# First products copied into the bank of the second product, gate rows on another engine, and loads and forms at other steps

## The chip, the cores and the metric

The kernel runs on one core of a Trainium2 chip. The core has a matrix engine (TensorE, PE in the profile; its weight loads are listed apart as PEld), a vector engine (VectorE, DVE), a scalar engine (ScalarE, ACT), GpSimd (POOL, used here to issue stores) and SyncE (SP, used here to issue loads). Each engine works through its own instruction queue; they wait for each other by semaphores. The metric is the time of one execution on the device in microseconds (us), the median of several runs.

## The reference, cut to what matters

```python
g = sigmoid((x * gate_w).sum(-1, keepdims=True))          # x: 2048 x 512
a = x @ hid_re.T ; b = x @ hid_im.T                       # hid: 512 x 512
fourier = seq_re @ a - seq_im @ b                         # seq: 2048 x 2048
swiglu = (silu(x @ w1) * (x @ w3)) @ w2                   # w1, w3: 512 x 1376
return g * fourier + (1 - g) * swiglu
```

All of it is float32.

## The kernel before, in words

**Products.** Each large product is taken as a 2 x 2 block product by seven block multiplications with sums of blocks in front and behind (a Strassen-Winograd scheme). Each float32 operand is split into a high part (rounded to fp32r, `high`, a ScalarE copy) and a low part (`low`, a VectorE subtraction: source minus high). One block product is then three matmuls: high x high, high x low, low x high (`mm3`, line 122). The first matmul of a product needs the high part of the moving operand, the second its low part.

**Stage one** (lines 345 to 405, to about 208 us) computes silu(x w1) and x w3 for 22 items n, an item being 128 of the hidden columns and one half of the rows of x. An item has seven products of six matmuls. X is the bank of the first product (weights `wa`, x form B11). The first and second products of item n + 3 are taken during item n (LOOK = 3): `first1` makes X, and ScalarE copies X into the SBUF tile s1 (`copy_x`, line 291). Two products later `first2` makes the second product in its own bank Y (one of two), VectorE adds Y to s1 (`sum_g`, line 305), and ScalarE applies Silu to s1 (`gate1`, line 309). The X bank keeps the first product and gets others added to it. The weights of the back half of the items are loaded a second time, `load_w` for `wa` and `load_wb` for `wb`; ScalarE makes the high part of `wa`, VectorE the low. Items 0 to 3 have a start written out by hand (lines 409 to 515).

The order of all instructions is the order in which the Python code is written; nothing reorders it. Functions are put into lists (`early`, `ahead`, `second`, `mid`, `at_end`) that `gate_up` runs at fixed points of an item.

**Stage two** (from line 627) has eight blocks: four of the Fourier product (kind F, 28 steps each), two of kind H (the product with w2, 21 steps) and two of kind Y (the hidden Fourier matrices, 14 steps). A step is a quarter, a third or a half of one of the seven products P1, P5, P6, P3, P7, P2, P4 and has twelve matmuls (six where half a form is empty). Its moving operand is the tile zo of that step (high and low). While TensorE works on step m, `advance(m)` issues the load for step m + 8, the sum (line 682 or 685) for step m + 4 and the split into zo for step m + 3. There are four zo tiles, so VectorE and ScalarE can be three steps ahead.

The stationary operands of the F blocks are forms of x: A1 (made in stage one) and A2, eight tiles a2_0 to a2_7, made from eight reloaded x tiles xs during block 0. For each p of them there is one subtraction of 128 x 256 (`sum2`, line 174), and a split of two parts: "first" forms (512 wide) and a "third" form (256 wide, from the result of that subtraction). P7 (steps 16 to 19) reads the third forms, P2 and P4 (steps 20 to 27) the first ones. In the kernel before, the subtraction for p stands at step 7 + p and the split of both parts at step 8 + p.

When a product ends its banks are read: P1 into s1, P5 into p5, P6 into u2, P7 into u3 by ScalarE; results of P3, P2, P4 and P7 are summed, multiplied with the gate by VectorE and stored (`spill`, from line 811). The P3 result of block 0 is worked off at step 18. The gate rows themselves (`gates`) are made from the scores at step 4 of block 0 and step 3 of block 1. Six matrices (two of w2, four of the hidden Fourier matrix) are turned into forms "late", two in each of blocks 1, 2 and 3 (`late_load`, `late_sums`, `late_split1`, `late_split2`), and stored to memory for blocks 4 to 7.

Of the kernel before, what the change touches and what calls it, by code (L numbers as in the profile page):

```python
# [7 lines left out]
F32 = mybir.dt.float32  # L8
# [20 lines left out]
A1_AT = (12, 14, 16, 17, 18, 19, 20)  # L29


@with_exitstack
def fnet_swiglu_gate_kernel(
# [142 lines left out]
    def forms2(r, t2):  # L176

        r = r.rearrange("p (a n) -> p a n", a=4)
        split(flat(t2[:, 0, 0:2]), flat(t2[:, 1, 0:2]), flat(r[:, 2:4]))
        split(t2[:, 0, 2], t2[:, 1, 2], r[:, 0])  # L180

# [99 lines left out]
    def first1(n):  # L281
        copy_x(n, prod1(n))
# [6 lines left out]
    def copy_x(n, x):  # L289
        s1 = s1p.tile([P, 512], F32, tag="s1", name=f"s1_{n}")  # L290
        nc.scalar.activation(s1, x, AF.Copy)
        G[n] = (x, s1)

    def first2(n):

        sum_g(n, prod2(n))

    def prod2(n):
        y = bank(4 + n % 2, f"Y{n}")
        prod(y, n, 1, 1, True)  # L300
        return y

    def sum_g(n, y):
        s1 = G[n][1]
        nc.vector.tensor_add(s1, s1, y)
        put_score(n, 0, s1)

    def gate1(n):
        nc.scalar.activation(G[n][1], G[n][1], AF.Silu)
# [35 lines left out]
    def gate_up(n):  # L345
# [17 lines left out]
        if wa in WA or wa == 0:  # L363
            wa = None
        else:
            load_w(wa, 0, 3 if back(wa) else 4)

# [44 lines left out]
    wps = bank(7, "wps")  # L412
# [82 lines left out]
    y1 = prod2(1)  # L495
    copy_x(1, x1)
    nc.vector.tensor_mul(h0[:, 512:], g1, C[1, 1])
    store_h(0, 1, h0[:, 512:])
    x2 = prod1(2)
    high_wb(1)  # L500
    sum_g(1, y1)
    y2 = prod2(2)
    low(*wa_parts(3, 0, 3))
    copy_x(2, x2)
    sum_xo(0, "T3", ST[0, "B12"])
    gate1(1)
    x3 = prod1(3)
    low_wb(1)
    high(*xo_parts(0, "T3")[::2])
    y3 = prod2(3)  # L510
    copy_x(3, x3)
# [12 lines left out]
    do(second, 1, sum_g, 2, y2)  # L524
    do(mid, 1, gate1, 2)
    do(early, 2, sum_g, 3, y3)
    do(mid, 2, gate1, 3)
# [200 lines left out]
    def load_a2(p):  # L728
# [5 lines left out]
        elif p < NG - 2:  # L734
            XR[p] = flat(ut.tile([P, 2, 512], F32, tag=("u3", "c21")[p % 2], name=f"xs{p}"))
# [13 lines left out]
    def load_score(g):  # L749
        t, ng = GATES[g] = [flat(ut.tile([P, 2, 512], F32, tag=k, name=f"{k}g{g}"))  # L750
                            for k in ("p5", "u2")]
# [8 lines left out]
    def gates(g):  # L760

        t, ng = GATES.pop(g)
        nc.scalar.activation(t, t, AF.Sigmoid)
        for j, (v, w) in enumerate(((-1.0, 1.0), (1.0, -1.0))):
            b = slice(j * 512, (j + 1) * 512)
            nc.vector.tensor_scalar(ng[:, b].rearrange("p (n a) -> p a n", a=2),
                                    t[:, b].rearrange("p (a n) -> p a n", a=2),
                                    v, w, op0=ALU.mult, op1=ALU.add)
        nc.scalar.activation(t[:, 512:], t[:, 512:], AF.Copy, scale=-1.0)
        nc.gpsimd.dma_start(gsp[g], t)  # L770
        nc.gpsimd.dma_start(ngsp[g], ng)
# [100 lines left out]

    def step(m):
# [4 lines left out]
        if q == 0 and k in ("P1", "P5", "P2"):  # L878
            banks = {"P1": XB[blk % 2], "P5": ZB, "P2": YB}[k]
            U[k] = [bank(b, f"{k}_{blk}_{r}") for r, b in enumerate(banks)]  # L880
# [3 lines left out]
        own = k in ("P1", "P5", "P2")  # L884
# [46 lines left out]
        if k == "P1":  # L931
# [5 lines left out]
        elif k == "P3":  # L937
# [4 lines left out]
            result() if blk else todo.setdefault(m + 3, []).append((result, ()))  # L942
        elif k == "P7":
# [6 lines left out]
            spill(blk, 3, U["p5"])  # L950
        elif k == "P2":
# [114 lines left out]
```

## Time and profile before

| | |
|---|---|
| median of the runs | 679.93 us (679.02, 679.96, 679.93) |
| span of the profiled execution, first to last instruction | 678.0 us |
| outside the span, median less span | 1.93 us |
| mean granted TensorE clock | 1.000 |
| PE / PEld / DVE / ACT / POOL busy | 671.4 / 583.1 / 601.9 / 367.1 / 64.0 us |
| memory traffic | 172.5 MB, mean 254 GB/s |

The profiled execution's own time is not listed apart from its span; the 1.93 us are taken as what lies around it. In the profile a line L122 is line 122 of the kernel; helpers give all their instructions one line (L108 all high parts, L111 all low parts, L122 all matmuls but the warm-up). A row of a timeline has start and duration in us, engine, line, operation, output<-input, size, count, and in square brackets the idle time before it and what ended it. A row of waits has the sum in us, how often, and the longest. A row of windows has, for PE, PEld, DVE, ACT and POOL, the busy time in us, then the granted clock, the share of the memory engines that was busy, and GB/s.

### The profile page before, as it was taken

The numbers are of one execution on the slowest core, as the hardware profiler recorded it, in microseconds if no ns is written. First come the engines' busy times: TensorE is split into PE (matmuls) and PEld (weight loads), VectorE is DVE, ScalarE is ACT, GpSimd is POOL, SyncE is SP. The second block draws the span as 40 slices with busy tenths as digits, with TensorE's granted clock in tenths as the row PEclk, the third lists the DMA queues.
The fourth block names the chain that finished last, engine by engine and source line by source line (L and its number), as shares of the span: only waits on it lengthen the run. The fifth ranks groups of instructions, "written<-read, shape, count | busy, mean of one in ns | idle before, by whom it ended". The sixth has DMA issues, their size and how long they took to land.

```text
span 678.0 us, 8653 instructions
## 1 busy us (share of the span) xinstructions
PE 671.4 (99%) x3101; PEld 583.1 (86%) x3101; DVE 601.9 (89%) x738; ACT 367.1 (54%) x480; POOL 64.0 (9%) x118
## 2 busy tenths in 40 slices
PE   9999999999999999999999999999999999999997
PEld 6888888888888888888888888888888888888886
DVE  6999988787679999987999799979998897898995
ACT  6665566654546754454554554555546455455452
POOL 0021112221010000000110001100110000000000
PEclk9999999999999999999999999999999999999999
DMA  7675557599998656912497238915999972874932
GB/s 294 218 294 219 219 203 267 198 325 380 415 418 295 242 189 232 339 64 93 165 380 278 94 105 332 376 58 199 373 418 417 414 272 90 310 284 153 336 127 93
DMA packets 45547, 172.54 MB, mean 254 GB/s; under 512 B 5312, under 2 KB 5696, under 8 KB 41664
## 3 DMA queue, kind: packets, MB, share of 16 engines
q1 hardware_dynamic: 32608, 118.63, 48.0%
q0 software_dynamic: 12608, 52.97, 19.6%
q8 instruction: 24, 0.39, 0.2%
q10 hardware_dynamic: 288, 0.39, 0.2%
q14 instruction: 19, 0.16, 0.1%
HBM read 114.82 MB, written 57.16 MB: 254 GB/s over the span
## 4 chain that ended last, share of the span: by engine, by line
PE 51%; issue 37%; DMA 7%; POOL 3%; DVE 1%; ACT 0%; POOLq 0%; SPq 0%; ACTq 0%; DVEq 0%
PE P L122 24%; PE X L122 14%; PE Z L122 7%; PE Y L122 3%; DMA B<-hsp 2%; PE C L122 2%; DMA dsp<-late_0l 2%; DMA ws<-w 1%; DMA hsp<-h 1%; POOL zsp L821 1%; DMA p5g<-gs 1%; PE wps L414 1%; POOL dsp L803 1%; POOL w2sp L803 1%; DVE zo L111 0%
## 5 line engine op out<-in xcount | busy, mean ns | idle before, releaser
L122 PE MATMUL P<-zo,a 128*128 128x512 f32 x1344 | 290.8, 379 | 1.0 <-DVE zo L111 1.0
L122 PEld LDWEIGHTS P<-zo,a 128*128 128x128 f32 x1344 | 253.7, 189 | 38.0 <-DVE zo L111 2.0
L108 ACT ACTIVATE zo<-B 128x1024 fp32r<-128x1024 f32 (+1 forms) x182 | 188.4, 1041 | 180.5 <-DVE B L682 83.5
L111 DVE TENSOR_TENSOR zo<-B,zo 128x1024 fp32r<-128x1024 f32 (+1 forms) x182 | 217.2, 1200 | 30.9 <-ACT zo L108 30.2
L122 PE MATMUL P<-zo,H 128*128 128x512 f32 x468 | 101.4, 379 | 0.5 <-DVE zo L111 0.5
L122 PEld LDWEIGHTS P<-zo,H 128*128 128x128 f32 x468 | 88.4, 189 | 13.4 <-DVE zo L111 0.9
L682 DVE TENSOR_TENSOR B<-B,B 128x1024 f32<-128x1024 f32 (+1 forms) x78 | 92.7, 1189 | 1.5 <-DMA B<-hsp 1.4
L122 PE MATMUL X<-xo,wb 128*128 128x512 f32 x378 | 88.7, 379 | 0.0
L122 PEld LDWEIGHTS X<-xo,wb 128*128 128x128 f32 x378 | 71.2, 189 | 10.6 <-DVE u L382 0.3
L122 PE MATMUL P<-zo,Y 128*128 128x512 f32 (+1 forms) x336 | 71.6, 375 | 0.0
L122 PEld LDWEIGHTS P<-zo,Y 128*128 128x128 f32 x336 | 62.7, 189 | 8.7
L334 POOL DMA_DIRECT2D hsp<-h x42 | 23.0, 548 | 120.5 <-DVE h L388 66.3
L685 DVE TENSOR_TENSOR B<-B,B 128x1024 f32<-128x1024 f32 x26 | 31.6, 1216 | 0.0
L122 PE MATMUL X<-xo,wa 128*128 128x512 f32 x126 | 31.0, 381 | 0.3 <-ACT h L399 0.3
L122 PE MATMUL Y<-xo,wa 128*128 128x512 f32 x126 | 30.6, 379 | 0.0
L122 PE MATMUL Z<-xo,wb 128*128 128x512 f32 x126 | 30.6, 379 | 0.0
L122 PE MATMUL Z<-xo,wa 128*128 128x512 f32 x126 | 30.6, 379 | 0.0
L111 DVE TENSOR_TENSOR wa<-ws,wa 128x768 fp32r<-128x768 f32 (+1 forms) x22 | 19.3, 880 | 11.0 <-ACT wa L108 11.0
L925 ACT ACTIVATE zu<-P 128x512 f32<-128x512 f32 x32 | 19.0, 596 | 17.3 <-PE P L122 15.7
L122 PEld LDWEIGHTS X<-xo,wa 128*128 128x128 f32 x126 | 23.6, 189 | 4.5 <-ACT h L399 0.7
L122 PEld LDWEIGHTS Y<-xo,wa 128*128 128x128 f32 x126 | 23.8, 189 | 3.4
L122 PEld LDWEIGHTS Z<-xo,wb 128*128 128x128 f32 x126 | 23.8, 189 | 3.4
(140 smaller groups left out, 549.0 us busy)
## 6 DMA issues: line engine op xcount, KB each, us to landing
B<-cc SPq DMA_DIRECT2D x64, 512.0 KB, 6.4
hsp<-h POOLq DMA_DIRECT2D x42, 256.0 KB, 3.7
B<-hsp SPq DMA_DIRECT2D x20, 512.0 KB, 10.8
wbsp<-wb POOLq DMA_DIRECT2D x8, 1024.0 KB, 4.2
wb<-wbsp SPq DMA_DIRECT2D x8, 1024.0 KB, 8.1
B<-zsp SPq DMA_DIRECT2D x16, 512.0 KB, 8.3
H<-w2sp SPq DMA_DIRECT2D x6, 1024.0 KB, 9.3
ws<-w SPq DMA_DIRECT2D x11, 512.0 KB, 4.7
```

Source lines behind the costliest of these rows:

```text
L108: nc.scalar.activation(hi, src, AF.Copy)
L111: nc.vector.tensor_sub(lo, src, hi.bitcast(F32))
L122: nc.tensor.matmul(ps.rearrange("p (n a) -> p n a", a=2), u, turns(v)[:, some], **kw)
L334: nc.gpsimd.dma_start(hsp[g, b + k, j // 2, :, j % 2 * 512 : (j % 2 + 1) * 512], h)
L414: nc.tensor.matmul(wps, warm[:, :P], warm, start=True, stop=True)
L682: nc.vector.tensor_add(t, t, RAW[blk, b, q][:, :n])
L685: nc.vector.tensor_sub(t, RAW[blk, "B12", q], t)
L803: nc.gpsimd.dma_start(flat(dst[:, k]), v[:, : 1024 - 256 * j].bitcast(F32))
L821: return nc.gpsimd.dma_start(z_rows(blk, k), flat(t))
L925: nc.scalar.activation(U[name][:, r], ps[r], AF.Copy)
```

## The change

1. *Seeds.* ScalarE's copy of the first product goes into the bank Y of the second product (`seed`), and the second product is accumulated on it. `sum_g`'s addition goes; `gate1` reads Y. At the start, items 1 to 3 are ordered X1, X2, Y1, X3, Y2, Y3, and the warm-up matmuls use the bank 5. In stage two the P1 result of blocks 0 to 6 is copied into the two banks of P2 in the same way and `plus("s1")` goes; the multiplication with the gate (in block 6 the addition of nb) reads the banks.
2. *Gate rows.* The two rows of 1 - g and g - 1 are made by ScalarE, and the five instructions are spread over four steps (steps 2 to 5 of block 0, 3 to 6 of block 1).
3. *x forms.* A table gives, for each p, the step of its load, of its subtraction with the third form, and of its first form: subtraction and third form of p now stand together at steps 8 to 11 and 13 to 16, the first forms at 8 to 11, 17, 18, 18 and 19. P3's result of block 0 moves from step 18 to step 24.
4. *Late matrices and weights.* Blocks 1 and 2 take three late matrices each and block 3 none. The weights `wa` of the back half are loaded one item sooner.

```diff
+A2_AT = ((4, 8, 8), (5, 9, 9), (6, 10, 10), (7, 11, 11),
+         (8, 13, 17), (9, 14, 18), (10, 15, 18), (11, 16, 19))
...
-    def copy_x(n, x):
+    def seed(n, x):
+        y = bank(4 + n % 2, f"Y{n}")
+        nc.scalar.activation(y, x, AF.Copy)
+        G[n] = (x, y)
+
+    def first2(n):
+        prod(G[n][1], n, 1, 1, False, True)
+
+    def gate1(n):
+        x, y = G[n]
         s1 = s1p.tile([P, 512], F32, tag="s1", name=f"s1_{n}")
-        nc.scalar.activation(s1, x, AF.Copy)
+        nc.scalar.activation(s1, y, AF.Silu)
+        put_score(n, 0, y)
         G[n] = (x, s1)
-
-    def first2(n):
-        sum_g(n, prod2(n))
...
-    def sum_g(n, y):
-        s1 = G[n][1]
-        nc.vector.tensor_add(s1, s1, y)
-        put_score(n, 0, s1)
...
+        ask = WSET[n + LOOK + 2] if n + LOOK + 1 < last else 0
+        if back(ask) and ask not in WS:
+            load_w(ask, 0, 3)
...
-    def make_a2(p):
+    def third_a2(p):
         A2.append(a2.tile([P, 2, 3, 256], F32R, tag=f"a2_{p}", name=f"a2_{p}"))
-        r = XR.pop(p)
-        forms2(r, A2[p])
-        if p >= NG - 2:
+        r, t = XR[p], A2[p]
+        sum2(r)
+        split(t[:, 0, 2], t[:, 1, 2], r[:, :256])
+
+    def first_a2(p):
+        r, t = XR.pop(p), A2[p]
+        split(flat(t[:, 0, 0:2]), flat(t[:, 1, 0:2]), r[:, 512:])
+        if p >= NG - 1:
             free(r)
...
+        elif i < 3:
+            v = (1.0, -1.0)[i - 1]
+            b = slice((i - 1) * 512, i * 512)
+            nc.scalar.activation(ng[:, b].rearrange("p (n a) -> p a n", a=2),
+                                 t[:, b].rearrange("p (a n) -> p a n", a=2),
+                                 AF.Copy, bias=v, scale=-v)
...
-        if k == "P1":
+        if k == "P1" and seeded:
+            new_banks("P2", blk)
+            for r in range(2):
+                nc.scalar.activation(U["P2"][r], ps[r], AF.Copy)
+        elif k == "P1":
             read("s1")
...
-            result() if blk else todo.setdefault(m + 3, []).append((result, ()))
+            result() if blk else todo.setdefault(m + 9, []).append((result, ()))
...
+        elif k == "P2" and seeded:
+            spill(blk, 0, res("s1"), ps)
         elif k == "P2":
             plus("s1")
             spill(blk, 0, U["s1"])
...
-    for p in range(NG):
-        at(0, 4 + p, load_a2, p)
-
-        at(0, 7 + p, lambda p=p: sum2(XR[p]))
-    for p in range(NG):
-        at(0, 8 + p, make_a2, p)
+    for p, (load, third, rest) in enumerate(A2_AT):
+        at(0, load, load_a2, p)
+        at(0, third, third_a2, p)
+        at(0, rest, first_a2, p)
...
-        blk, b = 1 + i // 2, i % 2
-        n = (17, 24)[b]
-        at(blk, n - (5, 6)[b], late_load, i, src[p], ("u3", "u2")[b])
+        blk, b = 1 + i // 3, i % 3
+        n = (10, 17, 24)[b]
+        at(blk, n - (6, 5, 6)[b], late_load, i, src[p], ("u3", "s1", "u2")[b])
```

Where instructions move, three places. The first is VectorE in block 0, at the x forms that stand before the splits of steps 15 to 17 (xs is a reloaded x tile, a2 its form, B11 <- B12, B11 the sum of T3, zo the low part of a step). Before:

```order
L174 TENSOR_TENSOR xs5_2114<-xs5_2114 128x256
L111 TENSOR_TENSOR a2_4_2186<-xs4_2089,a2_4_2186 128x512
L111 TENSOR_TENSOR a2_4_2186<-xs4_2089,a2_4_2186 128x256
L685 TENSOR_TENSOR B11_0_0_1654<-B12_0_0_1886,B11_0_0_1654 128x1024
L111 TENSOR_TENSOR zo15_2206<-B22_0_3_1979,zo15_2206 128x1024
L174 TENSOR_TENSOR xs6_2137<-xs6_2137 128x256
L111 TENSOR_TENSOR a2_5_2210<-xs5_2114,a2_5_2210 128x512
L111 TENSOR_TENSOR a2_5_2210<-xs5_2114,a2_5_2210 128x256
L685 TENSOR_TENSOR B11_0_1_1726<-B12_0_1_1914,B11_0_1_1726 128x1024
L111 TENSOR_TENSOR zo16_2230<-B11_0_0_1654,zo16_2230 128x1024
```

And after:

```order
L113 TENSOR_TENSOR zo15_2179<-B22_0_3_1959,zo15_2179 128x1024
L176 TENSOR_TENSOR xs4_2073<-xs4_2073 128x256
L113 TENSOR_TENSOR a2_4_2182<-xs4_2073,a2_4_2182 128x256
L672 TENSOR_TENSOR B11_0_1_1705<-B12_0_1_1893,B11_0_1_1705 128x1024
L113 TENSOR_TENSOR zo16_2201<-B11_0_0_1634,zo16_2201 128x1024
L176 TENSOR_TENSOR xs5_2098<-xs5_2098 128x256
L113 TENSOR_TENSOR a2_5_2204<-xs5_2098,a2_5_2204 128x256
L672 TENSOR_TENSOR B11_0_2_1759<-B12_0_2_1895,B11_0_2_1759 128x1024
L113 TENSOR_TENSOR zo17_2223<-B11_0_1_1705,zo17_2223 128x1024
```

The subtraction xs of a p moved from the step ahead to the place right before the low part of its own third form, and the 512-wide low parts moved behind step 19.

The second is ScalarE in block 0 at steps 11 to 13, the high parts of the x forms and of zo. Before:

```order
L108 ACTIVATE a2_0_2091<-xs0_2004 128x512
L108 ACTIVATE a2_0_2091<-xs0_2004 128x256
L108 ACTIVATE zo11_2110<-B12_0_3_1918 128x1024
L108 ACTIVATE a2_1_2116<-xs1_2030 128x512
L108 ACTIVATE a2_1_2116<-xs1_2030 128x256
L108 ACTIVATE zo12_2133<-B22_0_0_1920 128x1024
```

And after:

```order
L110 ACTIVATE a2_0_2067<-xs0_1986 128x256
L110 ACTIVATE a2_0_2067<-xs0_1986 128x512
L110 ACTIVATE zo11_2089<-B12_0_3_1897 128x1024
L110 ACTIVATE a2_1_2092<-xs1_2007 128x256
L110 ACTIVATE a2_1_2092<-xs1_2007 128x512
L110 ACTIVATE zo12_2112<-B22_0_0_1899 128x1024
```

The copy of 256, which reads the result of the subtraction, moved ahead of the copy of 512.

The third is TensorE at the start of stage one. Before:

```order
L122 MATMUL X1_234<-xo0_109,wa1_219 128x512 x6
L122 MATMUL Y1_249<-xo0_109,wa1_219 128x512 x6
L122 MATMUL X2_260<-xo0_109,wa2_222 128x512 x6
L122 MATMUL Y2_270<-xo0_109,wa2_222 128x512 x6
L122 MATMUL X3_282<-xo0_109,wa3_247 128x512 x6
```

And after:

```order
L124 MATMUL X1_234<-xo0_109,wa1_219 128x512 x6
L124 MATMUL X2_249<-xo0_109,wa2_222 128x512 x6
L124 MATMUL Y1_256<-xo0_109,wa1_219 128x512 x6
L124 MATMUL X3_273<-xo0_109,wa3_247 128x512 x6
L124 MATMUL Y2_269<-xo0_109,wa2_222 128x512 x6
```

The second product of an item moved one product back.

More of the change, by code (lines that the diff above doesn't have):

```diff
@@ L281, in first1 @@
     def first1(n):
-        copy_x(n, prod1(n))
+        seed(n, prod1(n))
     def prod1(n):
@@ L758, in fnet_swiglu_gate_kernel, with gates @@
     load_score(0)
[L760 to L771, printed above, removed]
+    def gates(g, i):
+        t, ng = GATES[g]
+        if i == 0:
+            nc.scalar.activation(t, t, AF.Sigmoid)
+        elif i < 3:
[4 more added lines that the diff above has]
+                                 AF.Copy, bias=v, scale=-v)
+        else:
+            nc.scalar.activation(t[:, 512:], t[:, 512:], AF.Copy, scale=-1.0)
+            nc.gpsimd.dma_start(gsp[g], t)
+            nc.gpsimd.dma_start(ngsp[g], ng)
     LATE = {}
@@ L871, in load_forms, with new_banks @@
         nc.sync.dma_start(t.bitcast(F32), sp[j][p])
+    def new_banks(k, blk):
+        banks = {"P1": XB[blk % 2], "P5": ZB, "P2": YB}[k]
+        U[k] = [bank(b, f"{k}_{blk}_{r}") for r, b in enumerate(banks)]
     def step(m):
@@ L883, in step @@
         z = zt.rearrange("p h a n -> p h (a n)")
-        own = k in ("P1", "P5", "P2")
+        own = k in ("P1", "P5") or k == "P2" and not seeded
         first = k in ("P1", "P5", "P6", "P3")
```

61 lines of the change are left out of this document (25 added, 36 removed).

## The prediction

> **What bounds the kernel now.** I read the page's busy times first, then what the TensorE weight loads waited for, then those waits in order of time, then VectorE and ScalarE around them. The head of the page:
>
> ```profile
> span 678.0 us, 8653 instructions
> PE 671.4 (99%) x3101; PEld 583.1 (86%) x3101; DVE 601.9 (89%) x738; ACT 367.1 (54%) x480; POOL 64.0 (9%) x118
> ```
>
> The chain of waits gives the pace of TensorE:
>
> ```profile
> 38.93 1.29 PE Z L122 x6
> ...
> 149.01 1.29 PE Y L122 x6
> ```
>
> From 38.93 to 149.01 are 85 products of six matmuls without a gap, 110.08 / 85 = 1.295 us each. So a step of stage two (twelve matmuls) is 2.59. TensorE is the bound, the change takes no matmul away, and only such gaps can be won. What weight loads waited for, and the later waits in order of time:
>
> ```profile
> PEld P L122 <- DVE zo L111: 2.9, 4, 1.1
> PEld X L122 <- ACT h L399: 0.7, 1, 0.7
> PEld C L122 <- ACT xo L108: 0.7, 1, 0.7
> PEld X L122 <- DVE wa L111: 0.5, 2, 0.3
> PEld X L122 <- DVE u L382: 0.3, 1, 0.3
> PEld X L122 <- DVE wb L111: 0.2, 1, 0.2
> ```
>
> ```profile
> 181.72 0.30 PEld L122 LDWEIGHTS X<-xo,wa 128*128 128x128 f32 x2 [0.74 <-ACT h L399]
> 249.42 2.46 PEld L122 LDWEIGHTS P<-zo,a 128*128 128x128 f32 x12 [0.19 <-DVE zo L111]
> 252.96 2.46 PEld L122 LDWEIGHTS P<-zo,a 128*128 128x128 f32 x12 [1.09 <-DVE zo L111]
> 256.17 43.90 PEld L122 LDWEIGHTS P<-zo,a 128*128 128x128 f32 x204 [0.75 <-DVE zo L111]
> 508.13 11.95 PEld L122 LDWEIGHTS P<-zo,H 128*128 128x128 f32 x56 [0.86 <-DVE zo L111]
> ```
>
> Between loads 0.03 is ordinary (2.59 / 12 - 0.19). Block 0 of stage two loses 0.16 + 0.95 + 0.62 = 1.73 (252.96 - 249.42 is 3.54 instead of 2.59; then 3.21), the start of block 4 0.83. Stage one's waits, h 0.7, wa 0.5, u 0.3 and wb 0.2 less 0.03 each, are 1.5 at most, partly hidden by the matmul before; I count 1.1, the half of what is short and the whole of 181.72. That is some 3.7 us in all. Why block 0 waits, and how full VectorE is there and in block 1:
>
> ```profile
> 208.00:281.00 73.00, 71.96 (x332) 62.16 (x331) 72.18 (x86) 44.97 (x59) 3.75 (x7) 1.00 0.72 252
> 281.00:353.00 72.00, 72.00 (x336) 63.04 (x335) 64.19 (x72) 37.28 (x45) 5.95 (x12) 1.00 0.50 187
> ```
>
> The third busy figure is VectorE: 72.18 of 73. Block 0 is its bound, the granted clock is 1.00, and ScalarE has 28 us free there. Block 1 has 7.8 us of VectorE free.
>
> **The seeds.** Here is the group of the old copy, then a copy and its second product at the latest place of stage one:
>
> ```profile
> L291 ACT ACTIVATE s<-X 128x512 f32<-128x512 f32 x21 | 12.5, 596 | 10.1 <-PE X L122 10.0
> ```
>
> ```profile
> 183.46 0.60 ACT L291 ACTIVATE s<-X 128x512 f32<-128x512 f32 x1
> ...
> 185.79 1.46 PE L122 MATMUL Y<-xo,wa 128*128 128x512 f32 x6
> ```
>
> 21 additions leave VectorE in stage one; no wait above names them, so TensorE loses nothing to them directly. The 21 copies stay where they were in ScalarE's queue but now TensorE waits for each. The copy ended at 184.06, 1.7 us ahead; the two products between first and second (2.59) are the cover. Writing PSUM instead of SBUF has no row; between ScalarE's rows of 256 (0.42) and of 1024 (1.05) it lies near its own 0.60, and at 1.05 it would still be 1.2 ahead: cost 0. If the cover went, what is lost would count 21 times. The gate's activation reads the bank in place of SBUF: no TensorE wait. In stage two seven blocks get the same, and the second product there starts 16 steps later: cost 0.
>
> The start of stage one is reordered (X1, X2, Y1 in the order shown ahead). VectorE drops three additions and moves the low half of wb1 ahead of T3's sum. The waits on wa, u and wb there shrink; T1's and T3's lows come later. I take -0.3, between -0.5 (all gone) and +0.3 (half an addition late). The weights of later c are asked for one iteration (9.1 us) sooner, one transfer moved ahead on SP's queue, past w2's and x's loads. The ScalarE row behind the wait at 181.72:
>
> ```profile
> 180.34 0.84 ACT L108 ACTIVATE wa<-ws 128x768 fp32r<-128x768 f32 x1 [3.99 <-DMA ws<-w]
> ```
>
> 3.99 is less than 9.1, so that wait goes: -0.6 (0.74 less 0.03, and a part hidden); between -0.7 and 0, since queues are full and another load may be late next.
>
> **Block 0.** The rows of VectorE, then of ScalarE, at the gate rows and the x forms (a<-xs):
>
> ```profile
> 221.74 0.84 DVE L766 TENSOR_SCALAR u2g<-p5g 128x512 f32<-128x512 f32 x2
> ...
> 224.28 1.23 DVE L111 TENSOR_TENSOR zo<-B,zo 128x1024 fp32r<-128x1024 f32 x1 [0.62 <-ACT zo L108]
> ...
> 231.43 1.22 DVE L111 TENSOR_TENSOR zo<-B,zo 128x1024 fp32r<-128x1024 f32 x1
> ...
> 234.98 0.41 DVE L174 TENSOR_TENSOR xs<-xs 128x256 f32<-128x256 f32 x1
> 235.31 1.02 DVE L111 TENSOR_TENSOR a<-xs,a 128x512 fp32r<-128x512 f32 x2
> 236.25 1.21 DVE L111 TENSOR_TENSOR zo<-B,zo 128x1024 fp32r<-128x1024 f32 x1
> 237.38 0.41 DVE L174 TENSOR_TENSOR xs<-xs 128x256 f32<-128x256 f32 x1
> ```
>
> ```profile
> 235.42 0.42 ACT L108 ACTIVATE a<-xs 128x256 fp32r<-128x256 f32 x1 [0.32 <-DVE xs L174]
> 235.75 1.05 ACT L108 ACTIVATE zo<-B 128x1024 fp32r<-128x1024 f32 x1
> ```
>
> *Saved:* the gate rows on VectorE (0.70 up to the next start) with the wait they caused (0.62), and one sum that goes behind zo10 (0.34): VectorE is 1.7 earlier at zo10. ScalarE takes two new gate rows in block 0 and two in block 1, about 0.6 each, in idle time before its zo copies (bounds 0.4 and 1.05, its rows of 256 and 1024): cost 0. A row of 512 takes 0.60 from start to start (235.31 to 236.25, less 0.34 for the 256), one of 1024 1.13 (236.25 to 237.38). Two additions of P2 (1.2) go too, and its multiplications now read PSUM. Rows of both kinds:
>
> ```profile
> L819 DVE TENSOR_TENSOR zs<-zs,gate 128x512 f32<-128x512 f32 x12 | 7.7, 681 | 0.0
> L819 DVE TENSOR_TENSOR zc<-P,gate 128x512 f32<-128x512 f32 x12 | 7.7, 680 | 0.0
> ```
>
> They cost the same: 0. [...]
>
> *Added:* a wait. Before, the sum xs of p+1 ran a step ahead of its copy. Now sum, ScalarE's copy of it and VectorE's low of it follow each other in one step. The row at 235.42 shows the hand-over: the sum of 234.98 ended at 235.39, the copy began 0.03 later. So the low of 256 starts 0.41 + 0.03 + 0.42 + 0.03 = 0.90 after the sum starts instead of 0.33, and VectorE idles 0.56. For p = 0 to 3 the copy of 512 and zo's copy stand behind it on ScalarE: 0.44 + 0.33 (235.42 to 235.75) + 0.51 (the 0.60 of a 512 copy, overlapped by 0.09 as there) + 1.05 = 2.33, so zo's low starts 2.36 after the sum, and the next sum at 2.36 + 1.13 = 3.5 (2.40 now, 234.98 to 237.38). For p = 4 to 6: 0.90 + 0.34 + 1.13 (sum of T3) + 1.13 = 3.5. Each such step is 0.91 over TensorE's 2.59.
>
> Step 16 was due at 249.26, so step 10 at 233.71; zo10 ended at 232.65, ahead by 1.06. Afterwards 1.06 + 1.7 = 2.8. Steps 11 to 14 use 4 x 0.91 = 3.65: TensorE waits 0.9 at step 14. Step 15 has no x form (two rows, 2.27) and gains 0.3. Steps 16 to 18 wait 0.6, 0.9, 0.9; step 19, without a T3 sum behind it but with zo19's copy late (copy from 0.77 to 1.82, low from 1.85 to its successor 2.98), 0.4. Then the four deferred lows fit into steps 20 to 22. Before zo27 stand P2's two multiplications (1.2) and now P3's two additions and two multiplications (2.4): steps 24 to 26 use 2.27, with lead 1.0; step 27 takes 2.27 + 3.6 - 1.13 = 4.74, 1.2 late. With 0.1 at step 23 the sum is 0.9 + 0.6 + 0.9 + 0.9 + 0.4 + 0.1 + 1.2 = 5.0, against 1.73: **+3.3**. Bounds: if ScalarE's wait cost half, 1.73 remains (0); if every step also lost a hand-over of 0.1, +4.5.
>
> [...]
>
> In the order shown ahead, the low of a2_4 now stands right behind its sum, with one sum of B11 and zo16 behind it.
>
> **Late matrices.** Blocks 1 and 2 take a third, some 3.5 us of VectorE each (six rows of 256 at 0.33, one of 512 at 0.6, one of 768 near 0.9), less P2's 1.2; block 1 has 7.8 free: 0, at most 1 each. Block 3 has none, and SP no longer waits ahead of block 4's forms. The wait at 508.13 comes from this, with memory traffic full:
>
> ```profile
> 480.00:490.00 10.00, 10.00 (x48) 8.77 (x47) 9.96 (x10) 3.73 (x4) 1.63 (x3) 1.00 1.01 419
> ```
>
> ```profile
> 502.25 1.23 DVE L682 TENSOR_TENSOR B<-B,B 128x1024 f32<-128x1024 f32 x1 [1.45 <-DMA B<-hsp]
> ```
>
> VectorE gains some 3.5 there and the load leaves earlier: -0.8 (bounds -0.83 and 0).
>
> **Sum.** 678.0 + 3.3 - 0.8 - 0.6 - 0.3 = 679.6. The median of the runs shown lies 1.9 above the span: **681.5 us**.
>
> **The rivals.** *Faster:* the wait within a step is hidden, because copies are ready sooner than I count; then VectorE's lead at zo10 (2.8) and the deferred lows wipe out block 0's 1.73: 679.9 - 1.7 - 1.7 = 676.5. For it speaks only that VectorE's own work falls. It decides if the step of an x form stays under 2.9 (lead 2.8 over seven steps, 0.3 each). 0.08. *Half:* block 0 as before, 678.2 to 680.4: 0.2. *Nothing else is won:* loads of w and hsp arrive as late as now: 679.9 + 3.3 = 683.2: 0.15. *Seeds late:* ScalarE waits for a weight past the 1.7 of cover; 0.5 at each of 21 would be 692; from 0.08 each it outweighs the gains. Of the idle time before the 21 old copies 10.0 of 10.1 us is for X, so they ran as soon as it was done: 0.03.
>
> **How the numbers follow.** My forecast has 0.54, with 680.6 to 682.5 of its own. A change of 0.2% (1.4 us) is about what a measurement here tells from none. Slower: two thirds of my case and the last two rivals, 0.54. Faster: the first rival and half of the second, 0.18. Same: 0.28. Range 678.2 to 683.3, from the half case to nothing else won.
>
> **What would show it.** Right: VectorE rows a<-xs of 256 with idle of about 0.55 released by ScalarE, waits of TensorE on zo from steps 14 to 19 and at 27 of some 5 us, none at 181 and 508, and no wait of Y on a seed. Wrong: no idle before those rows, or a gap at each Y product.

## The result and the profile after

The changed kernel takes 682.52 us, the median of four runs (682.33 to 683.34), beside 679.94 us for the kernel before (679.02 to 680.08): a ratio of 1.0045, with a 95% interval of 1.0031 to 1.0059. It is slower: by less than half a percent, but clear of the interval.

The head of its page, and then what the weight loads of TensorE waited for (us in all, how often, the longest), from an execution of 682.46 us:

```profile
span 680.7 us, 8593 instructions
PE 672.0 (99%) x3101; PEld 582.6 (86%) x3101; DVE 582.1 (86%) x700; ACT 369.1 (54%) x484; POOL 64.1 (9%) x118
```

```profile
PEld P L124 <- DVE zo L113: 6.0, 7, 1.3
```

VectorE lost 19.8 us of work (601.9 to 582.1) and TensorE waits more: the waits on zo grew from 2.9 to 6.0. The later waits in order of time; the number in brackets is the idle time before the row:

```profile
28.88 0.94 PEld L124 LDWEIGHTS X<-xo,wb 128*128 128x128 f32 x5 [0.67 <-DVE xo L113]
141.60 2.46 PEld L124 LDWEIGHTS X<-xo,wb 128*128 128x128 f32 x12 [0.41 <-DVE u L372]
244.95 5.04 PEld L124 LDWEIGHTS P<-zo,a 128*128 128x128 f32 x24 [0.94 <-DVE zo L113]
250.73 2.46 PEld L124 LDWEIGHTS P<-zo,a 128*128 128x128 f32 x12 [0.74 <-DVE zo L113]
254.25 2.46 PEld L124 LDWEIGHTS P<-zo,a 128*128 128x128 f32 x12 [1.06 <-DVE zo L113]
257.76 2.46 PEld L124 LDWEIGHTS P<-zo,a 128*128 128x128 f32 x12 [1.06 <-DVE zo L113]
260.75 10.22 PEld L124 LDWEIGHTS P<-zo,a 128*128 128x128 f32 x48 [0.53 <-DVE zo L113]
271.29 10.22 PEld L124 LDWEIGHTS P<-zo,a 128*128 128x128 f32 x48 [0.32 <-DVE zo L113]
282.84 219.80 PEld L124 LDWEIGHTS P<-zo,a 128*128 128x128 f32 x1019 [1.32 <-DVE zo L113]
```

The waits at 181.72 and 508.13 are gone. Seven waits stand in block 0. What a wait costs is better read from the distance of these rows than from the brackets, which come out larger: 254.25 - 250.73 is 3.52, so 0.93 over the 2.59 of a step, where the bracket says 1.06. The same reading gives 0.60 between 244.95 and 250.73 (two steps), then 0.93, 0.92, 0.40, 0.18 and 1.19. For the first wait, at step 14, the loads of steps 14 and 15 begin at 243.81 and 247.21, 3.40 apart: 0.81. The seven make 5.03. Before, the same reading gives 0.06, 0.95 and 0.62, in all 1.63.

To see where the 2.7 us of span come from, I compare the same weight loads in both traces. Before, then after:

```profile
43.74 1.27 PEld L122 LDWEIGHTS Z<-xo,wb 128*128 128x128 f32 x6
143.45 1.27 PEld L122 LDWEIGHTS Z<-xo,wb 128*128 128x128 f32 x6
207.59 4.51 PEld L122 LDWEIGHTS P<-zo,a 128*128 128x128 f32 x21
499.31 7.96 PEld L122 LDWEIGHTS P<-zo,H 128*128 128x128 f32 x37
672.41 1.42 PEld L122 LDWEIGHTS P<-zo,Y 128*128 128x128 f32 x12
```

```profile
44.10 1.27 PEld L124 LDWEIGHTS Z<-xo,wb 128*128 128x128 f32 x6
144.09 1.27 PEld L124 LDWEIGHTS Z<-xo,wb 128*128 128x128 f32 x6
207.54 4.52 PEld L124 LDWEIGHTS P<-zo,a 128*128 128x128 f32 x21
502.66 12.49 PEld L124 LDWEIGHTS P<-zo,H 128*128 128x128 f32 x58
675.04 1.42 PEld L124 LDWEIGHTS P<-zo,Y 128*128 128x128 f32 x12
```

| stretch | measured, after less before | forecast |
|---|---|---|
| start, to 44 us | +0.36 | -0.3 |
| stage one, to 144 us | 0.64 - 0.36 = +0.28 | 0 |
| rest of stage one, with the wait at 181 | -0.05 - 0.64 = -0.69 | -0.6 |
| blocks 0 to 3 | 3.35 + 0.05 = +3.40 | +3.3 |
| blocks 4 to 7 | 2.63 - 3.35 = -0.72 | -0.8 |
| sum | +2.63 | +1.6 |

Each column of rows is one execution; the traces of the experiments below show how far the stretches repeat. Blocks 0 to 3 do: 295.12 us here and 295.10 to 295.11 in the fifth, sixth and seventh experiment, 291.72 in the kernel before and in that kernel with the seeds alone. The small parts of stage one do not. The wait at 181 has 0.74, 0.44, 0.62, 0.74 and 0 us in five executions that load this weight at the later place. The wait at 141 stands in three of four executions that load as the changed kernel does. And 0.12 of the start's 0.36 is there before the new order begins: the first X product starts at 16.47 in place of 16.35, because the first x tile arrived later (ScalarE's first copy of it, released by the load, starts at 5.29 in place of 4.96).

VectorE in block 0, at the x forms of steps 9, 10, 13 and 14 (xs is the reloaded x tile, a its form):

```profile
234.28 0.42 DVE L176 TENSOR_TENSOR xs<-xs 128x256 f32<-128x256 f32 x1
235.18 1.22 DVE L113 TENSOR_TENSOR a<-xs,a 128x256 fp32r<-128x256 f32 x2 [0.48 <-ACT a L110]
236.64 1.23 DVE L113 TENSOR_TENSOR zo<-B,zo 128x1024 fp32r<-128x1024 f32 x1 [0.25 <-ACT zo L110]
237.79 0.42 DVE L176 TENSOR_TENSOR xs<-xs 128x256 f32<-128x256 f32 x1
...
247.08 0.42 DVE L176 TENSOR_TENSOR xs<-xs 128x256 f32<-128x256 f32 x1
247.98 0.43 DVE L113 TENSOR_TENSOR a<-xs,a 128x256 fp32r<-128x256 f32 x1 [0.48 <-ACT a L110]
...
250.59 0.42 DVE L176 TENSOR_TENSOR xs<-xs 128x256 f32<-128x256 f32 x1
```

From subtraction to subtraction are 3.51 us in both kinds of step, and VectorE sits idle behind each subtraction until ScalarE has copied its result. This is the wait that the forecast counts; the experiments test whether it is the cause of TensorE's waits.

### The profile page after: what moved, and what is told of

Read it like the earlier page. It is cut to its first block, busy times and chain, and to the rows that moved or that the text cites. A ratio compares the mean times of both kernels' runs of the same rounds, so it can differ in the third digit from the quotient of the medians.

```text
span 680.7 us, 8593 instructions
## 1 busy us (share of the span) xinstructions
PE 672.0 (99%) x3101; PEld 582.6 (86%) x3101; DVE 582.1 (86%) x700; ACT 369.1 (54%) x484; POOL 64.1 (9%) x118
## 3 DMA queue, kind: packets, MB, share of 16 engines
q0 software_dynamic: 12608, 52.97, 19.8%
## 4 chain that ended last, share of the span: by engine, by line
PE 84%; DVE 10%; issue 2%; DMA 2%; ACT 2%; SPq 0%; ACTq 0%; DVEq 0%
PE P L124 58%; PE X L124 15%; PE Z L124 8%; DVE zo L113 4%; PE Y L124 3%; DVE B L669 2%; DMA xs_B<-xt 1%; DMA B<-cc 1%; ACT zo L110 1%; DVE B L672 1%; DVE a L113 1%; DVE wa L113 1%; DVE xs_B L207 1%; ACT a L110 0%; DVE xs L176 0%
## 5 line engine op out<-in xcount | busy, mean ns | idle before, releaser
L389 ACT ACTIVATE h<-X 128x512 f32<-128x512 f32 x20 | 11.9, 597 | 30.5 <-PE X L124 30.2
L124 PEld LDWEIGHTS Z<-xo,wa 128*128 128x128 f32 x126 | 23.8, 189 | 3.4
```

Source lines behind the costliest of these rows:

```text
L124: nc.tensor.matmul(ps.rearrange("p (n a) -> p n a", a=2), u, turns(v)[:, some], **kw)
L389: nc.scalar.activation(g1, x, AF.Silu)
```

## The experiments

Two theories of block 0 stood against each other. *Lock-step*: subtraction, ScalarE's copy and VectorE's low in one step make VectorE late. *Other moves*: gate rows on ScalarE, the seeds, and P3's result at step 24 do it. All times are medians; ratios are to runs of the kernel before in the same session, whose medians were 679.50 (first four experiments), 679.55 (the next four), 679.67 (the three behind those) and 679.64 us (the last). Where an experiment is set against the changed kernel's 682.52 us, two sessions are compared, and the kernel before itself moved by up to 0.4 us between them; the traces decide where less than that is at stake.

### The subtraction one step ahead

```diff
     def third_a2(p):
...
-        sum2(r)
...
         at(0, load, load_a2, p)
+        at(0, third - 1, lambda p=p: sum2(XR[p]))
```

> The changed kernel, with each subtraction of an x tile put one step ahead of the split of its third form, as it stood before the change; everything else stays. Lock-step theory (sum, ScalarE's copy and VectorE's low within one step make block 0 late): the rows a<-xs of 256 no longer wait 0.48 for ScalarE, a step of steps 8 to 11 costs VectorE about 2.4 and one of steps 13 to 16 about 2.94 in place of 3.51; nearly all of block 0's 5.8 us of TensorE waits go, those at steps 23 and 27 too since VectorE comes there with a lead: 676.9 us, between 676.5 and 677.5. Rival (the other moves make block 0 late: gate rows on ScalarE, seeds, P3's result at step 24): at least half of the 5.8 stays, 679.6 or more.

Measured: 677.36 us (677.26 to 677.91), ratio 0.9967 (0.9955 to 0.9980); 5.2 less than the changed kernel. VectorE at the same steps:

```profile
233.52 0.41 DVE L176 TENSOR_TENSOR xs<-xs 128x256 f32<-128x256 f32 x1
233.86 1.01 DVE L113 TENSOR_TENSOR a<-xs,a 128x256 fp32r<-128x256 f32 x2
...
235.93 0.41 DVE L176 TENSOR_TENSOR xs<-xs 128x256 f32<-128x256 f32 x1
```

No idle time is left, the step takes 2.41 in place of 3.51, and the waits of TensorE name no zo any more. All of block 0's waits go with this one move, those at steps 23 and 27 included, so none of the other moves makes them without it. In the trace blocks 0 to 3 take 290.09 us, 5.03 less than in the changed kernel. The 0.5 between the measured time and the forecast is a wrong price: I added up the brackets of the seven waits (5.8) where their distances give 5.03. Stage one ends at the same time in both traces (207.55 and 207.54). This execution lacks the wait at 141 and has another, 0.55 at 183, on a copy of ScalarE that waited 2.26 for the store of h.

### P3's result back at step 18

```diff
-            result() if blk else todo.setdefault(m + 9, []).append((result, ()))
+            result() if blk else todo.setdefault(m + 3, []).append((result, ()))
```

> The changed kernel, with P3's result of block 0 back at step 18 in place of 24; everything else stays. Lock-step theory: VectorE is already late at step 18, so the 2.4 us of the result are lost there, less the 0.3 that each of steps 20 to 22 has to spare; the waits of 1.3 at step 27 and 0.3 at step 23 go: about +0.5, 683.0 us, between 682.5 and 683.6. Rival (the later place of the result is itself a loss): the wait at step 27 goes and nothing takes its place, 681.0.

Measured: 683.63 us (683.00 to 683.88), ratio 1.0055 (1.0042 to 1.0069): 1.1 slower than the changed kernel, 0.03 above the upper end of the lock-step theory, and not the 1.5 faster of the rival. The wait at step 27 is gone, a wait stands at step 21, where there was none, and the one at step 23 has grown; both have 1.43:

```profile
267.35 5.05 PEld L124 LDWEIGHTS P<-zo,a 128*128 128x128 f32 x24 [1.43 <-DVE zo L113]
273.82 230.16 PEld L124 LDWEIGHTS P<-zo,a 128*128 128x128 f32 x1067 [1.43 <-DVE zo L113]
```

I had set 0.9 us of slack in steps 20 to 22 against the 2.4. In the changed kernel that slack is already spent: on step 23, which is 0.18 late even so. By their distances the two waits cost 1.29 each, 2.58 together, which is the 0.18 and the whole 2.4; with the 1.19 of step 27 gone, 1.2 more are lost than before.

### The lock-step alone in the kernel before

```diff
-        split(flat(t2[:, 0, 0:2]), flat(t2[:, 1, 0:2]), flat(r[:, 2:4]))
         split(t2[:, 0, 2], t2[:, 1, 2], r[:, 0])
+        split(flat(t2[:, 0, 0:2]), flat(t2[:, 1, 0:2]), flat(r[:, 2:4]))
...
         r = XR.pop(p)
+        sum2(r)
         forms2(r, A2[p])
...
         at(0, 4 + p, load_a2, p)
-        at(0, 7 + p, lambda p=p: sum2(XR[p]))
```

> The kernel before, with each subtraction put directly ahead of the split of its third form, and this split ahead of that of the first forms; the steps stay 8 to 15. Lock-step theory: each of eight steps costs VectorE some 1.1 us more (0.56 of idle ahead of the low part and 0.5 ahead of zo's) and VectorE has nothing to spare there: 8.8 us more, 688.7 us, between 686 and 689.5. Rival (the place of the subtraction costs nothing, other moves made block 0 late): within 0.5 us of 679.9.

Measured: 687.08 us (686.38 to 688.14), ratio 1.0110 (1.0096 to 1.0124): 7.6 more than before. VectorE, two steps without and two with a sum of T3:

```profile
239.08 0.42 DVE L174 TENSOR_TENSOR xs<-xs 128x256 f32<-128x256 f32 x1
239.98 1.21 DVE L111 TENSOR_TENSOR a<-xs,a 128x256 fp32r<-128x256 f32 x2 [0.48 <-ACT a L108]
...
242.59 0.42 DVE L174 TENSOR_TENSOR xs<-xs 128x256 f32<-128x256 f32 x1
...
246.09 0.42 DVE L174 TENSOR_TENSOR xs<-xs 128x256 f32<-128x256 f32 x1
247.04 1.21 DVE L111 TENSOR_TENSOR a<-xs,a 128x256 fp32r<-128x256 f32 x2 [0.53 <-ACT a L108]
...
250.45 0.42 DVE L174 TENSOR_TENSOR xs<-xs 128x256 f32<-128x256 f32 x1
```

A step takes 3.51 without that sum and 4.36 with it. Without the lock-step they took 2.40 and, in the trace before from 245.75 to 249.29, 3.54: 1.11 and 0.82 more. Four of each make 7.7, and 7.6 were measured. My 8.8 counted 1.1 in every step; where a sum stands between the forms and zo, it covers the wait for zo's copy.

### The seeds alone in the kernel before

```diff
     def first1(n):
-        copy_x(n, prod1(n))
+        x = prod1(n)
+        y = bank(4 + n % 2, f"Y{n}")
+        nc.scalar.activation(y, x, AF.Copy)
...
     def first2(n):
-        sum_g(n, prod2(n))
+        prod(G[n][1], n, 1, 1, False, True)
...
-        if k == "P1":
+        if k == "P1" and seeded:
+            new_banks("P2", blk)
+            for r in range(2):
+                nc.scalar.activation(U["P2"][r], ps[r], AF.Copy)
+        elif k == "P1":
...
+        elif k == "P2" and seeded:
+            spill(blk, 0, res("s1"), ps)
```

> The kernel before, with the seeds alone: first products copied into the bank of the second for items 4 to 21 of stage one, and P1 into the banks of P2 in blocks 0 to 6; the start and all else stay as before. Theory that the seeds cost nothing and win nothing: VectorE's busy time falls by about 19 us (18 and 14 additions of 0.6), the waits of TensorE stay the same, 679.9 us, within 0.5. Rival seeds late: Y products wait for ScalarE, 0.08 or more each, 681.4 or more. Rival relief (VectorE's work counts): 679.2 or less.

Measured: 680.38 us (679.73 to 680.97, 11 runs), ratio 1.0012 (1.0003 to 1.0021). VectorE's busy time falls by 17.7 us, and the time does not fall: it is 0.9 us more, 0.2 to 1.4 by the interval. So the theory is right that nothing is won, and its time of 679.9 was too good by up to that much. Block 0's three waits stand where they stood, to 0.03 us. The copies cost no Y product a wait but one of 0.24 at the start. What there is of a loss I can place in part: the load of hsp (the stored h) for block 4 lands at 502.58 in place of 502.25 although SyncE issues it at the same time, VectorE waits 2.52 for it in place of 1.45, and TensorE is 0.33 later there:

```profile
502.58 1.22 DVE L694 TENSOR_TENSOR B<-B,B 128x1024 f32<-128x1024 f32 x1 [2.52 <-DMA B<-hsp]
```

VectorE had got to that sum earlier and waited longer: at this place its work was never the bound. Whether the rest of the 0.9 is the seeds' or the scatter of that load stays open.

### The weights loaded as before

```diff
-        elif wa not in WS:
+        else:
             load_w(wa, 0, 3 if back(wa) else 4)
-        ask = WSET[n + LOOK + 2] if n + LOOK + 1 < last else 0
-        if back(ask) and ask not in WS:
-            load_w(ask, 0, 3)
```

> The changed kernel, with the weights wa loaded at the item at which the kernel before loads them; everything else stays. Queue theory (the earlier load of w stands on SP's queue waiting for its buffer, and the load of w2 behind it comes late): VectorE's wait of 2.0 us for w2r at 139 goes, and with it TensorE's wait of 0.4 on u at 141.6 (0.3 of it counts), but the wait on wa at 181 comes back with 0.7: 682.9 us. Rival (neither wait hangs on that load): 682.5 with the wait at 141 in place and none at 181.

Measured: 682.85 us (682.42 to 683.59), ratio 1.0048 (1.0034 to 1.0061). The median cannot tell the theory from the rival; the trace can. The wait at 181 is back:

```profile
182.19 0.30 PEld L124 LDWEIGHTS X<-xo,wa 128*128 128x128 f32 x2 [0.74 <-ACT h L386]
```

The wait at 141 is gone, and so is VectorE's wait for w2r, which the changed kernel has, shown here with SyncE's queue a little earlier. The changed kernel:

```profile
131.05 0.33 SPq L224 DMA_DIRECT2D ws<-w  x1
131.48 1.18 SPq L532 DMA_DIRECT2D w2r<-w  x1
```

```profile
139.27 0.43 DVE L152 TENSOR_TENSOR w2m<-w2r 128x256 f32<-128x256 f32 x1 [2.01 <-DMA w2r<-w]
```

Without the early load, w2r is issued at 128.44. With it, the load of ws stands ahead in SyncE's queue until 131.05, when its buffer is free (SyncE waited 18.0 for VectorE's last sum from it); w2r leaves at 131.48, arrives late, and the sum u that stands behind it on VectorE makes TensorE wait. One load moved ahead pays with another that stands behind it.

How much TensorE sees of either is less sure than the two waits behind them. In all five executions with the later load of that weight (this one, the kernel before, and its variants in the third, fourth and tenth experiment) ScalarE waits 4.0 to 5.0 us for it at 180, and TensorE 0 to 0.74. With the earlier load VectorE waits 2.0 us for w2r in three executions and TensorE 0.4; in the first experiment VectorE waits 1.66 and TensorE not at all.

### Two moves: the start, and the early load behind that of w2

```diff
-        ask = WSET[n + LOOK + 2] if n + LOOK + 1 < last else 0
-        if back(ask) and ask not in WS:
-            load_w(ask, 0, 3)
...
         run(at_end, n)
+        ask = WSET[n + LOOK + 2] if n + LOOK + 1 < last else 0
+        if back(ask) and ask not in WS:
+            load_w(ask, 0, 3)
...
+    sum_xo(0, "T3", ST[0, "B12"])
     low_wb(1)
     x3 = prod1(3)
     gate1(1)
-    sum_xo(0, "T3", ST[0, "B12"])
```

> The changed kernel, with two moves that lie far apart in the trace: the early load of wa stands at the end of its item, behind the loads of w2, and at the start VectorE's sum of T3 stands ahead of the low part of wb1. Queue theory: the wait at 141 goes (0.3) and the one at 181 stays away. Theory for the start (the high part of T3 stands on ScalarE behind the seed of item 3, which waits for X3, and VectorE's 1.1 us of idle behind it makes T1's low part late for the product at 28.9): that wait of 0.6 goes. Together 681.6 us. Rival for the start (data arrive later from memory): the wait at 28.9 stays, 682.2.

Measured: 681.61 us (681.48 to 681.84), ratio 1.0029 (1.0017 to 1.0040). The waits at 28.9, 141 and 181 are all gone; w2r leaves at 127.90 and ws at 130.58. At the start of the changed kernel ScalarE's queue had this order (Y<-X is the seed of item 3, xo the high part of T3; T1 and T3 are sums of x tiles), and VectorE behind it an idle time of 1.12 ahead of the low part of T3:

```profile
22.02 0.58 ACT L285 ACTIVATE Y<-X 128x512 f32<-128x512 f32 x1 [0.33 <-PE X L124]
23.38 1.06 ACT L110 ACTIVATE xo<-xs_B 128x1024 fp32r<-128x1024 f32 x1 [0.77 <-DVE xs_B L207]
```

```profile
24.46 1.22 DVE L113 TENSOR_TENSOR xo<-xs_B,xo 128x1024 fp32r<-128x1024 f32 x1 [1.12 <-ACT xo L110]
```

My reason was half right. The high part did not wait for the seed, which ended at 22.60; it waited 0.77 for VectorE's sum of T3, and then VectorE for it. It is the same pattern as in block 0: sum, copy and low of one tile directly behind one another. With the sum moved ahead the 1.12 are 0.25.

### Two late matrices in each of blocks 1 to 3

```diff
-        blk, b = 1 + i // 3, i % 3
-        n = (10, 17, 24)[b]
-        at(blk, n - (6, 5, 6)[b], late_load, i, src[p], ("u3", "s1", "u2")[b])
+        blk, b = 1 + i // 2, i % 2
+        n = (17, 24)[b]
+        at(blk, n - (5, 6)[b], late_load, i, src[p], ("u3", "u2")[b])
```

> The changed kernel, with two late matrices in each of blocks 1, 2 and 3 at the steps of the kernel before. Theory: the wait of TensorE at the start of block 4, on zo after a late load of hsp, comes back with 0.8: 683.3 us, and block 0 stays as it is. Rival (that wait went for another reason): 682.5.

Measured: 683.95 us (683.72 to 684.17), ratio 1.0064 (1.0052 to 1.0076): 1.4 more than the changed kernel. At the start of block 4 stand two waits, behind one of 2.71 of VectorE for hsp:

```profile
508.55 2.46 PEld L124 LDWEIGHTS P<-zo,H 128*128 128x128 f32 x12 [0.67 <-DVE zo L113]
512.02 92.89 PEld L124 LDWEIGHTS P<-zo,H 128*128 128x128 f32 x431 [1.01 <-DVE zo L113]
```

The move of the late matrices is what took the wait away, by the loads: in the changed kernel SyncE begins to issue the main run of eight loads of hsp at 470.13, here at 486.58. In the trace blocks 4 to 7 take 1.42 us more than in the changed kernel, so the size was off by 0.6. Counted from the start of block 4, the sum that needs the load starts here 3.63 us later and in the kernel before 2.94, though the loads are issued at the same distance; why the load lands later is open.

### The three mended

The moves of the first and of the sixth experiment together:

```diff
+        at(0, third - 1, lambda p=p: sum2(XR[p]))
...
+    sum_xo(0, "T3", ST[0, "B12"])
     low_wb(1)
...
         run(at_end, n)
+        ask = WSET[n + LOOK + 2] if n + LOOK + 1 < last else 0
```

> The changed kernel, with each subtraction one step ahead of its split, the early load of wa at the end of its item, and the sum of T3 ahead of the low part of wb1. Theory: the waits of block 0 (5.8 us), of 141 (0.3) and of 28.9 (0.6) go together: 676.0 us, faster than both kernels. Rival (another wait takes the place of those removed, in block 0 or 1): 677.5 or more.

Measured: 676.46 us (676.27 to 676.74), ratio 0.9953 (0.9941 to 0.9965): 6.1 less than the changed kernel, 3.1 less than the kernel before. The span is 674.7 us. None of the waits of its weight loads is later than 18.87 us. Behind the warm-up the longest are:

```profile
PEld C L124 <- ACT xo L110: 0.6, 1, 0.6
PEld Y L124 <- ACT Y L285: 0.5, 1, 0.5
```

Beside them stands one of 0.2 for an x tile, also at the start. The first product begins at 5.34 and the last matmul ends at 670.62. Between them the distances of the products show 0.7 us of waits, all ahead of 21 us; so next to nothing is left to win there without taking matmuls away. Here too the forecast's 676.0 was too low by the brackets of block 0, 5.8 where the distances give 5.0.

### The first seed ahead of a copy

```diff
-    high(*wa_parts(3, 0, 3)[::2])
     x2 = prod1(2)
     seed(1, x1)
+    high(*wa_parts(3, 0, 3)[::2])
```

> The mended kernel (subtraction one step ahead, early load of wa at the end of its item, sum of T3 ahead of the low part of wb1), with the seed of item 1 on ScalarE ahead of the high part of wa 3. Theory (the first seed has one product of cover, not two, and stands behind a copy of 0.84): the wait of Y of 0.47 at 18.9 goes, 0.2 to 0.5 of it counts, 676.1 us. Rival (the copy put back makes the third X product late): 676.5 or more.

Measured: 676.63 us (676.45 to 676.81), ratio 0.9953 (0.9940 to 0.9965), the ratio of the mended kernel. The wait of Y at 18.9 is gone from the trace, and from the first product to 44 us this execution is 0.3 us shorter; but its first product starts at 5.88 in place of 5.34, after a wait of 1.71 for ScalarE's copy of the x tile in place of 0.61. The medians of five executions each show nothing won, and the theory's 676.1 is not borne out. No third X product is late, as the rival had it.

### The gate rows alone in the kernel before

```diff
-            nc.vector.tensor_scalar(ng[:, b].rearrange("p (n a) -> p a n", a=2),
-                                    t[:, b].rearrange("p (a n) -> p a n", a=2),
-                                    v, w, op0=ALU.mult, op1=ALU.add)
+            nc.scalar.activation(ng[:, b].rearrange("p (n a) -> p a n", a=2),
+                                 t[:, b].rearrange("p (a n) -> p a n", a=2),
+                                 AF.Copy, bias=v, scale=-v)
...
-    at(0, 4, gates, 0)
+            at(g, n + i * (g == 0), gates, g, i)
```

> The kernel before, with the gate rows made by ScalarE, spread over steps 2 to 5 of block 0 (in block 1 all in step 3, as before). Theory: VectorE comes 1.3 us earlier (0.70 of work and 0.62 of wait) to step 10 of block 0, and 1.3 of the 1.7 us that TensorE waits in block 0 go: 678.2 us. Rival (ScalarE's two added rows make the next zo late): block 0 waits as before or more, 679.5 or more.

Measured: 678.28 us (677.40 to 679.18, 11 runs), ratio 0.9978 (0.9969 to 0.9987). Of block 0's three waits one of 0.34 is left, and blocks 0 to 3 take 290.30 us in place of 291.72: 1.42 less. (This execution also lacks the wait at 181, which no edit here touches, and has one of 0.54 at 28 in its place.) This part of the change is worth 1.4 us. Of the three parts tried alone in the kernel before, the lock-step, the seeds and the gate rows, it is the only gain. In the forecast the 1.3 of it were part of the lead of 2.8.

### P3's result at step 18 in the mended kernel

```diff
-            result() if blk else todo.setdefault(m + 9, []).append((result, ()))
+            result() if blk else todo.setdefault(m + 3, []).append((result, ()))
```

> The mended kernel, with P3's result of block 0 back at step 18. Theory: VectorE reaches step 18 with a lead that the four lows of 512 wide forms and the result's 2.4 us together use up or nearly: 0 to 0.7 us of waits, 676.5 to 677.2. Rival (the later place of the result is what the mended kernel lives on): two us or more are lost, 678.5 or more.

Measured: 676.67 us (676.57 to 676.77), ratio 0.9953 (0.9941 to 0.9966): no wait in block 0. Where VectorE has a lead, the place of the result costs nothing.

### Seven seeds in place of one

```diff
     def first1(n):
-        seed(n, prod1(n))
+        x = prod1(n)
+        seed(n, x)
+        for _ in range(6):
+            nc.scalar.activation(G[n][1], x, AF.Copy)
```

> The mended kernel, with the seed of each of items 4 to 21 written seven times over in place of once: ScalarE's copy takes some 3.0 us longer (six starts 0.5 apart). Cover theory (a seed ends 1.8 us before its Y product is due; beyond that the delay counts in full, for each item): 1.2 us for each of 18 items, 21.6 more than the 676.5 of the mended kernel: 698 us, between 694 and 704 since ScalarE's later copies are late too. Rival without cover (TensorE waits for every bit of the copy): 18 x 3.0, 730 us. Rival ample cover (ScalarE has 300 us free and TensorE doesn't notice): 677 us.

Measured: 713.45 us (713.37 to 715.26, 4 runs), ratio 1.0497 (1.0479 to 1.0514): 37 more than the mended kernel, 2.05 for each of 18 items. ScalarE and TensorE in one item:

```profile
108.18 0.58 ACT L288 ACTIVATE Y<-X 128x512 f32<-128x512 f32 x1 [0.70 <-PE X L124]
108.79 3.65 ACT L278 ACTIVATE Y<-X 128x512 f32<-128x512 f32 x6
```

```profile
109.27 1.46 PE L124 MATMUL Z<-xo,wa 128*128 128x512 f32 x6
112.49 1.56 PE L124 MATMUL Y<-xo,wa 128*128 128x512 f32 x6 [1.76 <-ACT Y L278]
```

The last copy ends at 112.44 and Y starts at 112.49. It was due at 109.27 + 1.295 = 110.57, and the first copy had ended at 108.76: the cover is 1.8 us. The copies cost 3.68, so 1.9 of each is seen, and the Y product itself takes 0.1 longer (1.56 in place of 1.46). The same 1.8 stands between seed and Y product in the changed kernel, in every item from item 6 on. The time lies outside my 694 to 704, because I took 0.5 from start to start where the row shows 0.61; with that, the cover theory gives 1.97 for each item, 712 us, while no cover would give 18 x 3.68, 743 us, and ample cover 677. The theory of the cover holds, and neither of the rivals does.

## Why the prediction was right, point by point

**Block 0, +3.3 forecast, +3.4 measured.** The forecast named waits of 0.9, 0.6, 0.9, 0.9, 0.4, 0.1 and 1.2 at steps 14, 16, 17, 18, 19, 23 and 27. The rows after, by their distances, give 0.81, 0.60, 0.93, 0.92, 0.40, 0.18 and 1.19. These are 5.03 against the 5.0 of the forecast; before, they are 1.63 where I had 1.73, since I read the first wait from its bracket (0.16) and its distance gives 0.06. The idle time behind the subtraction was 0.48 where I had 0.56, and the one ahead of zo's low 0.25; the step took 3.51 as worked out, with ScalarE's rows in the order written: idle 1.63 ahead of the x form's copies at 234.73, and zo's copy behind them at 235.57. That this is the cause, and not only beside it, is shown by taking it away (5.2 us less, 5.03 of it in block 0) and by adding it alone to the kernel before (7.6 us more). In the rival "faster" a slip stands: a lead of 2.8 over seven steps is 0.4 each, so the step should have been held against 3.0 and not 2.9; at 3.51 it decides the same.

**Seeds, 0.** Nothing is won by them, as forecast, though VectorE works 17.7 us less, and from item 6 on the copies end 1.8 us before they are needed. That they cost nothing is shown only in part: alone they made the kernel 0.9 us slower (0.2 to 1.4), and of this the trace places 0.3, on a load that came later. The multiplication of P2's result now reads the bank and took 679 ns, as forecast, against 681 before.

**Gate rows, 0 on ScalarE.** The cover was right and the price wrong: a row took 867 ns, not 0.6, inside the bounds of 0.4 and 1.05. Its output is written with a stride, which the x forms of 512 (615 ns) are not, nor is the gate row that is only negated (621 ns).

```profile
L761 ACT ACTIVATE u2g<-s1g 128x512 f32<-128x512 f32 x4 | 3.5, 867 | 0.0
```

**Weights, -0.6 forecast, -0.69 measured, and +0.28 not forecast.** "Queues are full and another load may be late next" stood as the bound of that term; it should have been a term. The load of w2 stood behind the one moved ahead, on a queue whose head waits for a buffer (131.05). How well -0.69 fits is in part luck: with the later load that wait was between 0 and 0.74 in five executions.

**The start, -0.3 forecast, +0.36 measured.** This is the step that failed. The old waits went as I had counted: by the distances of TensorE's products, those on u, wb and wa at 32.0, 33.7 and 36.5 had cost 0.37. But two new ones cost 0.63, and 0.12 is the late x tile. I took off VectorE's additions and did not follow the order of the two engines through the new sequence: the sum of T3, its high part and its low part came to stand directly behind one another, VectorE lost 1.12, and the T1 low that follows was late at 28.9 (0.67 in the bracket, 0.53 by distance). The first seed cost 0.10 at 19.1, with one copy of 0.84 ahead of it and 1.3 of cover less than the others. The lead that would have been needed was in the order shown ahead; I applied the lock-step rule to block 0 alone. The lead before was small, too. In the run with the gate rows alone, whose start is that of the kernel before, the T1 low is late as well:

```profile
28.26 0.94 PEld L122 LDWEIGHTS X<-xo,wb 128*128 128x128 f32 x5 [0.54 <-DVE xo L111]
```

It is late in two of four executions with the old order, in all five with the new one, and in none of the five with the sum of T3 moved ahead.

**Late matrices, -0.8 forecast, -0.72 measured.** Right, and by the load more than by VectorE: in the profile after, no wait stands at block 4, and in the run with the seeds alone VectorE came earlier and only waited longer.

So the time was 1.0 us higher than forecast, in the traces 0.94 of it from the start (0.66) and stage one (0.28). It lies at the upper end of the 680.6 to 682.5 that I had given the forecast. The rival "nothing else won" (683.2) lies nearer to 682.52 than the forecast's 681.5, but its reasons are not what happened: both waits that it kept were gone.

## What to carry to other kernels

When two engines work on one tile in turn (sum, copy, low), put each hand-over a step apart; in one step it cost the waiting engine the other's time though that other was idle for much of it (ScalarE 1.63 in a step of 3.51), here 1.1 us in a step of 2.6. Work taken from an engine counts only where that engine is waited for at that place: 18 us less of VectorE's work was worth nothing, 1.3 at the right place 1.4. Take the price of a wait from the distance between rows; the brackets added up to 5.8 us where 5.0 was lost. Before a load is moved ahead, read what stands behind it on its queue and whether its buffer is free by then: here w2r left at 131.48 in place of 128.44.

## What the runs showed of the hardware that I had not expected

The copies of ScalarE in the last experiment, which all read one bank and write another, follow each other 0.61 us apart (3.65 for six), while two that write different places start 0.49 apart, as here in the changed kernel:

```profile
181.72 0.60 ACT L359 ACTIVATE h<-X 128x512 f32<-128x512 f32 x1 [1.17 <-DMA hsp<-h]
182.21 0.59 ACT L363 ACTIVATE u<-Z 128x512 f32<-128x512 f32 x1
```

The rows at 181.72 and 182.21 overlap by 0.11. The copies from one bank to one other do not overlap at all: one takes 582 ns, less than the 0.61 between two starts. That they write to a bank is not the whole reason: the two seeds of P2 at 219.4, from two banks to two others, take 1.06 together and start 0.52 apart. Whether it is the same target or the same source is not separated.

The gate rows, written with a stride of two elements, took ScalarE 867 ns against 615 to 621 for 512 elements written in a row. They also add a bias, which the others do not, so that the stride is the reason is likely and not shown. The same rows on VectorE, in the kernel before, took 479 ns.
